# Twelve weight sums made in another part of a batch, with their loads at another place in the DMA queue

## The chip, the core and the metric

One core of a Trainium2 chip runs the whole program. The metric is the device time of one launch in microseconds. In the texts PE is TensorE (PEld its weight loads), DVE is VectorE, ACT is ScalarE, POOL is GpSimd and SP is SyncE, whose queue issues all the DMA transfers of this kernel.

## What is computed

Four batches of causal attention with a memory term, then two gated blocks of matrix products without any nonlinearity between the first block's last two matrices:

```python
scores = scale * q @ k.T, causal; a = softmax(scores); local = a @ v
mem = (phi(q) @ M_prev) / (phi(q) @ z_prev)
x  = g * mem + (1 - g) * local            # [2304, 512], 576 rows a batch
h  = (x @ w1) * (x @ w2)                  # 512 -> 1024
x2 = h @ (w3 @ w_out)                     # 1024 -> 512; the product W' of the two is made once
h  = sigmoid(x2 @ w_gate) * (x2 @ w_val)  # 512 -> 1536
y  = h @ w_out2                           # 1536 -> 512
```

## The kernel before, in words

A batch goes through four stages of matrix products on PE, and each stage is named by the tile in PSUM that it fills: `ab` (x @ w1 and x @ w2), `xw` (h @ W'), the gate stage (`gv` in batch 0, `gvp` in the others) and `ot` (the last product). `ab` runs over eight groups of 128 columns of h (f = 0 to 7), `xw` over four groups d, the gate over twelve, `ot` over four. Each 32-bit operand is split in a high and a low part and every product is made of three matmuls. While PE works on the products of batch b, the attention of batch b + 1 is laid between them: scores (`s`), softmax rows `p` in five row blocks i for each of four head pairs, transposes (`t`), and the products with v and the memory (`o`). In a name such as p2_0_1_0 the numbers are batch, head pair, row block, head. A row block goes from PE (`s`) to DVE (the row minimum and the masked copy, line 724), ACT (exp, line 107), DVE (reciprocal of the sum, lines 747 and 748), DVE and POOL (scaling, line 750, one head each) and back to PE (`t`, line 780), which then has ACT copy the transposed block out of PSUM. In `ab`, DVE multiplies the two halves of h (`hraw`, line 519), and ACT and DVE or POOL split the result into `h`.

The weights go through a ring of five slots (`wslot`). In batch 0 they are converted from 64 bits, and the split weights are stored to HBM (`k<-wslot`, line 328). From batch 1 on `load_step` loads them from there (`wslot<-k`, line 297); a load waits until PE has used up the slot's last weights.

In batches 1 to 3 the gate stage uses a scheme that multiplies sums of weight blocks: `two_rows` takes four slots for each of its twelve column groups, two of which hold sums that have to be made once. That is the making: for each of the twelve groups `load_kept` loads the raw weights that were kept in HBM (`wagain<-kf`, line 249, 512 KB, one of three buffers), and `make_step` makes four adds and subtractions on DVE (lines 265 to 268, 128 x 256 each), and then, for each of two halves, a cast on ACT and a subtraction on DVE (`wmade`, lines 456 and 458) and a store (`s<-wmade`, line 276). The gate stage of batch 1 loads the first sum right after the weights of `xw`. Making happens in batch 1 alone.

`pump`, which every stage calls once for each group of six matmuls or so, moves all this on: one step of conversion, one of loading or splitting, and, in batch 1 (`phase["n"] == 2`), at every second call one step of the making. The first of these steps loads the first three raw blocks at once; when a sum is finished, the load of the third next is issued. Whatever is left is made ahead of the last group of `xw`.

PE's instructions stand in the order in which the program is written. On DVE, ACT, POOL and SP the framework's scheduler sets the order when the program is built, by priority (the order of writing) and by its own idea of when an instruction's inputs are there; on the chip each engine then works strictly in that order, and SP issues its transfers in order too. Such an order puts instructions of the making ahead of the place where they were written when it believes the engine to be free. So the first `wagain` loads stand in SP's queue while PE is still at `ot` of batch 0.

Of the kernel before, what the change touches and what calls it, by code (L numbers as in the profile page):

```python
# [7 lines left out]
F32 = mybir.dt.float32  # L8
# [44 lines left out]
def tile_attention_memory_ffn(  # L53
# [17 lines left out]
    nc = tc.nc  # L71
# [21 lines left out]
    def lower(share):  # L93
        owed[share] = owed.get(share, 0.0) + share[phase["n"]]
        if owed[share] >= 1.0:
            owed[share] -= 1.0
            return nc.gpsimd
        return nc.vector
# [28 lines left out]
    kept = {}  # L127
# [45 lines left out]
    makes = [x[2] for x in seven[1::4]]  # L173
# [9 lines left out]
    ws = {"conv": 0, "step": 0, "split": 0, "ring": 0, "freed": 0, "use": 0, "again": 0, "mstep": 0, "pumps": 0, "wo": 0, "pass": 0, "wready": False}  # L183
    tmp = {}

    last = {}
# [56 lines left out]
    fresh = {}  # L243
    made = set()

    def load_kept(k):
        if k < len(makes):
            t = fp.tile([128, 8, 128], F32, tag="wraw", name=f"wagain{k}", bufs=3)
            nc.sync.dma_start(out=t, in_=kept[makes[k]])
            fresh[k] = t  # L250

    def make_step():


        k = len(made)
        if k >= len(makes):
            return False
        if ws["mstep"] == 0:
            if k == 0:
                assert not raws  # L260
                for n in range(3):
                    load_kept(n)
            a11, a12, a21, a22 = (fresh[k][:, 2 * n : 2 * n + 2] for n in range(4))
            e1, e2 = lower(SHARE_S), lower(SHARE_S)
            e1.tensor_add(a22, a21, a22)
            e2.tensor_sub(a21, a11, a21)
            e1.tensor_sub(a11, a22, a11)
            e1.tensor_sub(a12, a12, a11)
            ws["mstep"] = 1
            return True  # L270
        m = ws["mstep"] - 1
        t = fp.tile([128, 2, 4, 128], F32R, tag="r64", name=f"wmade{k}_{m}", bufs=R64)
        src = fresh[k].rearrange("p (a b) c -> p a (b c)", b=2)
        src = src[:, 0::3] if m == 0 else src[:, 1:3]
        split_rows(t.rearrange("p x (a b) c -> p x a (b c)", b=2), src, SHARE_W)
        nc.sync.dma_start(out=summed[makes[k]][m], in_=t.bitcast(F32))
        ws["mstep"] = (ws["mstep"] + 1) % 3
        if m == 1:
            made.add(makes[k])
            del fresh[k]  # L280
            load_kept(k + 3)
        return True

    def load_step():
        m = ws["again"]
        if m >= len(again):
            return False
        src, nb, u = again[m]
        late = m - NSECOND
        tag, bufs = ("wslot", RING) if late < 0 or late % (RING + 3) < RING else ("wraw", 3)  # L290
        if sum(places[x] == tag for x in slots) >= bufs:
            return False
        while u is not None and u not in made:
            make_step()
        n = ws["ring"]
        w = fp.tile([128, 2, 4, 128], F32R, tag=tag, name=f"wslot{n}", bufs=bufs)[:, :, :nb]
        nc.sync.dma_start(out=w.bitcast(F32), in_=src)
        slots[n] = w
        places[n] = tag
        ws["ring"] += 1  # L300
        ws["again"] += 1
        return True

    def split_step():
        s = ws["split"]
        if s >= 2 * NU:
            return load_step()
        if s >= ws["conv"]:
            return False
        u, hf = divmod(s, 2)  # L310
        r = raws[u][:, 4 * hf : 4 * hf + 4, :]
        if not units[u][1]:
            if ws["wo"] == 4 and ws["pass"] == 0:
                return False
            m = ws["wo"]
            t = fp.tile([128, 2, S], F32R, tag=f"h{8 + m % 4}", name=f"wo{m}", bufs=1)
            wot[m] = t
            split_rows(t[:, :, :DM].rearrange("p x (a c) -> p x a c", c=128), r, SHARE_W)
            ws["wo"] += 1
        else:  # L320
            if ws["ring"] >= ws["freed"] + RING:
                return False
            n = ws["ring"]
            w = fp.tile([128, 2, 4, 128], F32R, tag="wslot", name=f"wslot{n}", bufs=RING)
            split_rows(w, r, SHARE_W)
            if s in stored:
                nb = stored[s].shape[2]
                nc.sync.dma_start(out=stored[s], in_=w[:, :, 4 - nb :].bitcast(F32))
            slots[n] = w
            places[n] = "wslot"  # L330
            ws["ring"] += 1
        if hf == 1:
            del raws[u]
        ws["split"] += 1
        return True

    def pump():
        conv_step()
        split_step()
        if phase["n"] == 2:  # L340
            ws["pumps"] += 1
            if ws["pumps"] % 2 == 0:
                make_step()

    def need(store, s):
# [66 lines left out]
    def two_rows(s, x, name, ht, hraw):  # L412
# [4 lines left out]
        def product(n, sl, blk, xo):  # L417
            ps = ps_f.tile([128, 512], F32, tag="f", name=f"{name[:2]}p{name[2:]}_{n}")[:, :HS]
            prod2(ps, slot(s + sl), blk, x[xo])
            pump()  # L420
            return ps
# [33 lines left out]
    def split_rows(dst, src, share=None):  # L455
        nc.scalar.copy(dst[:, 0], src)  # L456
        eng = lower(share) if share else nc.vector
        eng.tensor_sub(dst[:, 1], src, dst[:, 0].bitcast(F32))  # L458

    def prep(g):  # L460
# [6 lines left out]
        for f in (f0, f0 + 1):  # L467
            s = take(1)
            if p == 1:
                part = fp.tile([128, DM], F32, tag="hraw", name=f"wpart{f}")  # L470
                nc.sync.dma_start(out=part, in_=wp[:, f])
            ps = ps_f.tile([128, 512], F32, tag="f", name=f"wps{p}_{f}")
            for m in range(4):
                prod(ps, slot(s), m, wot[4 * p + m], 0, m == 0, m == 3, n=DM)
                pump()
                yield 5.3
            release(s)
            if p == 0:
                st = fp.tile([128, DM], F32, tag="hraw", name=f"wst{f}")
                nc.scalar.copy(st, ps)  # L480
                nc.sync.dma_start(out=wp[:, f], in_=st)
            else:
                nc.vector.tensor_add(part, ps, part)
                nc.sync.dma_start(
                    out=wd[:, :, f, :], in_=part.rearrange("p (k c) -> p k c", c=128)
                )
# [5 lines left out]
    def ffn(b):  # L492
# [34 lines left out]
        for d in range(KC):  # L527
            while b == 1 and d == KC - 1 and make_step():
                pass
# [525 lines left out]
```

## Time and profile before

| | us |
|---|---|
| median of three runs | 1082.76 |
| fastest and slowest of them | 1078.57, 1084.03 |
| the profiled execution | 1079.02 |
| its span, first instruction to last | 1077.2 |

The profile is of one execution, 1079.02 us long, of which the span of 1077.2 us is what the rows below divide up. Batch 1's `ab` begins at 403.44 us of the span and its `xw` at 490.82. A row of a timeline merges instructions of one line that follow each other; the value in brackets is the idle time of the engine before the row, with what the profile holds for its releaser. Where an engine waited for several things, the profile names the one that came last, and where that one had long been done it was another. A row's time includes the pipeline's tail, so rows that follow each other can overlap.

### The profile page before, as it was taken

The numbers are of one execution on the slowest core, as the hardware profiler recorded it, in microseconds if no ns is written. First come the engines' busy times: TensorE is split into PE (matmuls) and PEld (weight loads), VectorE is DVE, ScalarE is ACT, GpSimd is POOL, SyncE is SP. The second block draws the span as 40 slices with busy tenths as digits, with TensorE's granted clock in tenths as the row PEclk, the third lists the DMA queues.
The fourth block names the chain that finished last, engine by engine and source line by source line (L and its number), as shares of the span: only waits on it lengthen the run. The fifth ranks groups of instructions, "written<-read, shape, count | busy, mean of one in ns | idle before, by whom it ended". The sixth has DMA issues, their size and how long they took to land.

```text
span 1077.2 us, 20188 instructions
## 1 busy us (share of the span) xinstructions
PE 1037.2 (96%) x7400; PEld 922.1 (86%) x7400; DVE 566.3 (53%) x1359; ACT 547.4 (51%) x1188; POOL 429.8 (40%) x373
## 2 busy tenths in 40 slices
PE   7999889999999998999999999999999999999998
PEld 3555667888999897888899899889999899999998
DVE  6854867755557557884555404453566301216630
ACT  7876767657767734564533424454544412224420
POOL 6966656426567602332533212332434200034320
PEclk9999999999999999999999999999999999999999
DMA  8674787858999589994688555433599455548981
GB/s 281 206 232 135 221 284 252 268 198 294 312 331 340 192 295 385 338 333 136 215 303 306 195 161 178 143 105 121 191 318 338 133 154 186 171 150 296 326 288 54
DMA packets 92667, 252.13 MB, mean 234 GB/s; under 512 B 11544, under 2 KB 30104, under 8 KB 92568
## 3 DMA queue, kind: packets, MB, share of 16 engines
q1 hardware_dynamic: 92568, 250.84, 68.3%
q8 instruction: 59, 0.97, 0.4%
q14 instruction: 40, 0.33, 0.1%
HBM read 194.70 MB, written 56.10 MB: 233 GB/s over the span
## 4 chain that ended last, share of the span: by engine, by line
PE 67%; DMA 6%; DVE 3%; POOL 2%; issue 2%; ACT 1%; SPq 1%; POOLq 0%; DVEq 0%; ACTq 0%
PE ab L372 17%; PE gvp L383 15%; PE ot L372 11%; PE xw L372 9%; PE gv L372 4%; PE s L719 3%; PE t L780 3%; PE o L848 2%; DMA wslot<-s 2%; DMA wagain<-kf 1%; PE o L833 1%; POOL x L458 1%; DMA wslot<-k 1%; PE o L841 1%; POOL wraw L234 1%
## 5 line engine op out<-in xcount | busy, mean ns | idle before, releaser
L372 PE MATMUL ab<-x,wslot 128*128 128x288 f32 x1536 | 232.6, 303 | 6.2 <-ACT asb L516 3.1
L372 PEld LDWEIGHTS ab<-x,wslot 128*128 128x128 f32 x1536 | 210.6, 191 | 18.2 <-issue 10.2
L383 PE MATMUL gvp<-x,wslot 128*128 128x288 f32 x1512 | 205.6, 296 | 7.8 <-POOL x L458 3.6
L383 PEld LDWEIGHTS gvp<-x,wslot 128*128 128x128 f32 x1512 | 202.1, 188 | 10.9 <-POOL x L458 4.5
L750 POOL TENSOR_SCALAR p<-p,sm,omg 116x116 f32<-116x116 f32 (+4 forms) x100 | 87.8, 881 | 203.5 <-DVE sm L748 139.6
L372 PE MATMUL ot<-hg,wslot 128*128 128x288 f32 x1152 | 163.4, 298 | 1.4 <-DVE hg L458 1.3
L372 PEld LDWEIGHTS ot<-hg,wslot 128*128 128x128 f32 x1152 | 154.1, 188 | 7.9 <-issue 5.1
L107 ACT ACTIVATE p<-p,sm 116x116 f32<-116x116 f32 (+4 forms) x160 | 93.2, 583 | 66.8 <-DVE sm L724 65.3
L724 DVE CUSTOM_DVE_ANT_0 p<-s,msk 116x116 f32<-116x116 f32 (+4 forms) x160 | 68.2, 453 | 108.5 <-PE s L719 108.3
L234 POOL TENSOR_TENSOR wraw<-wraw,cr 128x512 int32<-128x512 int32 x76 | 110.0, 1461 | 29.6 <-DVE wraw L230 27.9
L372 PE MATMUL xw<-h,wslot 128*128 128x288 f32 x768 | 111.6, 299 | 1.2 <-DVE h L458 0.9
L372 PEld LDWEIGHTS xw<-h,wslot 128*128 128x128 f32 x768 | 103.3, 188 | 4.9 <-issue 2.5
L372 PE MATMUL gv<-x,wslot 128*128 128x288 f32 x576 | 78.4, 296 | 2.0 <-DVE hgraw L584 1.4
L372 PEld LDWEIGHTS gv<-x,wslot 128*128 128x128 f32 x576 | 76.6, 188 | 3.6 <-DVE hgraw L584 2.5
L780 PE MATMUL t<-idf,p 116*116 116x116 f32 x480 | 71.0, 276 | 6.5 <-ACT qts L813 2.2
L780 PEld LDWEIGHTS t<-idf,p 116*116 116x116 f32 x480 | 55.6, 141 | 22.1 <-POOL p L750 5.8
L519 DVE TENSOR_TENSOR hraw<-ab,asb 128x288 f32<-128x288 f32 x64 | 29.2, 456 | 77.7 <-PE ab L372 71.9
L458 POOL TENSOR_TENSOR wslot<-wraw,wslot 128x512 fp32r<-128x512 f32 x36 | 47.4, 1316 | 54.3 <-ACT wslot L456 52.4
L221 ACT ACTIVATE cy<-r 128x512 f32<-128x512 f32 x76 | 50.1, 673 | 25.1 <-DVE wraw L230 10.1
L433 POOL TENSOR_TENSOR u4gv<-u2gv,s5gv 128x288 f32<-128x288 f32 x36 | 30.1, 836 | 69.5 <-ACT s5gv L431 69.5
L222 ACT ACTIVATE cr<-r 128x512 int32<-128x512 uint32 x76 | 50.9, 671 | 12.3 <-POOL wraw L234 11.7
L458 DVE TENSOR_TENSOR wslot<-wraw,wslot 128x512 fp32r<-128x512 f32 x40 | 48.6, 1214 | 15.9 <-ACT wslot L456 13.0
(108 smaller groups left out, 1459.4 us busy)
## 6 DMA issues: line engine op xcount, KB each, us to landing
wslot<-k SPq DMA_DIRECT2D x144, 512.0 KB, 4.4
wslot<-s SPq DMA_DIRECT2D x72, 512.0 KB, 4.6
k<-wslot SPq DMA_DIRECT2D x48, 512.0 KB, 4.4
r<-in_gv_dram SPq DMA_DIRECT2D x24, 512.0 KB, 5.5
s<-wmade SPq DMA_DIRECT2D x24, 512.0 KB, 6.1
qk<-in_qk_dram SPq DMA_DIRECT2D x32, 290.0 KB, 4.3
wslot<-k SPq DMA_DIRECT2D x36, 256.0 KB, 3.9
r<-in_w3t_dram SPq DMA_DIRECT2D x16, 512.0 KB, 4.7
```

The source lines that it names most:

```text
L107: ins = nc.scalar.activation(**kw)
L221: nc.scalar.activation(out=y, in_=hi, func=AF.Prelu, scale=2.0**-112, alpha=2.0**32)
L222: nc.scalar.activation(out=r, in_=w[:, :, 0].bitcast(U32), func=AF.Copy, scale=2.0**-29)
L234: nc.gpsimd.tensor_tensor(z, z, tmp["r"], ALU.add)
L372: nc.tensor.matmul(ps, w[:, wi, blk, :], x[:, xi, cols : cols + n], start=first and part == 0, stop=last and part == 2,)
L383: nc.tensor.matmul(ps, w[:, wi, blk + k, :], x[:, xi, k, :], start=k == 0 and part == 0, stop=k == 1 and part == 2,)
L433: nc.gpsimd.tensor_add(u4, u2, s5)
L458: eng.tensor_sub(dst[:, 1], src, dst[:, 0].bitcast(F32))
L719: nc.tensor.matmul(os_[hh], q_[r, 0, i * T : (i + 1) * T], k_[r, 1, c0:c1], start=x == 0, stop=x == len(terms) - 1,)
L724: nc.vector.tensor_tensor_reduce(out=ps_[hh][:, c0:c1], in0=os_[hh], in1=msk[:, SP - w + c0 : SP - w + c1], scale=-0.125, scalar=3.0e38 if ...
L750: lower(SHARE_N).tensor_scalar(ps_[hh][:, :w], ps_[hh][:, :w], sm[:, 6 + hh : 7 + hh], omg[:T, 2 * p + hh : 2 * p + hh + 1], ALU.mult, ALU ...
L780: nc.tensor.transpose(tp[:T, c : c + T], src[hh][:, j * T : (j + 1) * T], idf[:T, :T])
```

## The change

Three things are changed in the making, and nothing in what is computed. The step is called at 39 of the 88 calls of `pump` in batch 1's `ab` and the first three groups of `xw`, evenly, where it was every second call. The first three loads are steps of their own, one a step (39 = 3 + 12 x 3). And a making load is tied behind the latest ring load (`issue_after`), so that it stands after it in SP's queue.

```diff
     def load_kept(k):
         if k < len(makes):
             t = fp.tile([128, 8, 128], F32, tag="wraw", name=f"wagain{k}", bufs=3)
-            nc.sync.dma_start(out=t, in_=kept[makes[k]])
+            with tc.issue_after(last["ring"].ins):
+                nc.sync.dma_start(out=t, in_=kept[makes[k]])
             fresh[k] = t
...
         if ws["mstep"] == 0:
-            if k == 0:
+            if len(fresh) < 3 and k == 0:
                 assert not raws
-                for n in range(3):
-                    load_kept(n)
+                load_kept(len(fresh))
+                return True
...
-        nc.sync.dma_start(out=w.bitcast(F32), in_=src)
+        last["ring"] = nc.sync.dma_start(out=w.bitcast(F32), in_=src)
...
             ws["pumps"] += 1
-            if ws["pumps"] % 2 == 0:
+
+            if ws["pumps"] * 39 // 88 > (ws["pumps"] - 1) * 39 // 88:
                 make_step()
```

How the built order moves is seen at three places. In the names the number after a tile's own is the program's count of allocations, and lines after line 249 are one or two higher in the changed kernel.

SP's queue where batch 0 ends and batch 1's `ab` gets its first weights. Here `out_0_dram` is batch 0's result, `k79` and the like are split weights on their way to HBM, and `wslot76` and `wslot77` are the first two slots of `ab`. Before:

```order
L328 DMA k82_179<-wslot74_4635 128x1024
L249 DMA wagain2_4853<-kf26_121 128x1024
L276 DMA s25_0_117<-wmade1_0_5002 128x1024
L249 DMA wagain3_4929<-kf27_126 128x1024
L276 DMA s25_1_118<-wmade1_1_5021 128x1024
L297 DMA wslot76_4709<-k18_85 128x1024
L328 DMA k83_180<-wslot75_4693 128x1024
L249 DMA wagain4_5025<-kf28_131 128x1024
L297 DMA wslot77_4723<-k19_86 128x1024
L604 DMA out_0_dram<-osb0_2_4641 128x576
```

And in the changed kernel, from the same store on:

```order
L329 DMA k82_179<-wslot74_4635 128x1024
L298 DMA wslot76_4709<-k18_85 128x1024
L329 DMA k83_180<-wslot75_4693 128x1024
L298 DMA wslot77_4723<-k19_86 128x1024
L606 DMA out_0_dram<-osb0_2_4641 128x576
L298 DMA wslot78_4779<-k22_87 128x1024
L298 DMA wslot79_4793<-k23_88 128x1024
L298 DMA wslot80_4807<-k26_89 128x1024
L606 DMA out_0_dram<-osb0_3_4727 128x576
L250 DMA wagain0_4865<-kf24_111 128x1024
L250 DMA wagain1_4902<-kf25_116 128x1024
```

All five ring loads and the last store of batch 0 now stand ahead of the first making load, where there were five making loads and four stores of half sums ahead of the second ring load.

DVE in the first column group of batch 1's `ab`, from the product of the first half of h to the scaling of the second softmax row block (`p2_0_1_0`), for which PE's transposes wait. Before, the last nine rows of that stretch:

```order
L657 TENSOR_SCALAR me2_1_5289<-qnr2_1_5223 116x640
L748 RECIPROCAL sm2_0_1_4880<-sm2_0_1_4880 116x2
L265 TENSOR_TENSOR wagain5_5125<-wagain5_5125 128x256
L666 RECIPROCAL mn2_0_4839<-mn2_0_4839 116x10
L724 ISA p2_0_2_0_4937,sm2_0_2_4939<-s2_0_2_0_0_4940,msk_82 116x348
L724 ISA sm2_0_2_4939 116x1
L724 ISA p2_0_2_1_4938,sm2_0_2_4939<-s2_0_2_0_1_4941,msk_82 116x348
L724 ISA sm2_0_2_4939 116x1
L750 TENSOR_SCALAR p2_0_1_0_4878<-p2_0_1_0_4878,sm2_0_1_4880,omg_84 116x232
```

The same rows in the changed kernel:

```order
L659 TENSOR_SCALAR me2_1_5265<-qnr2_1_5205 116x640
L266 TENSOR_TENSOR wagain1_4902<-wagain1_4902 128x256
L268 TENSOR_TENSOR wagain0_4865<-wagain0_4865 128x256
L750 RECIPROCAL sm2_0_1_4872<-sm2_0_1_4872 116x2
L668 RECIPROCAL mn2_0_4839<-mn2_0_4839 116x10
L726 ISA p2_0_2_0_4921,sm2_0_2_4923<-s2_0_2_0_0_4924,msk_82 116x348
L726 ISA sm2_0_2_4923 116x1
L726 ISA p2_0_2_1_4922,sm2_0_2_4923<-s2_0_2_0_1_4925,msk_82 116x348
L726 ISA sm2_0_2_4923 116x1
L267 TENSOR_TENSOR wagain1_4902<-wagain1_4902 128x256
L269 TENSOR_TENSOR wagain0_4865<-wagain0_4865 128x256
L752 TENSOR_SCALAR p2_0_1_0_4870<-p2_0_1_0_4870,sm2_0_1_4872,omg_84 116x232
```

The whole stretch held one half sum (`wmade4_0`) and one add of `wagain5`; it now holds four adds of `wagain0` and two of `wagain1`, the first right behind `hraw1_0`. From that scaling on, up to the first instruction of the fifth row block (`p2_0_4_0`), there were seven adds and three half sums, and now there are ten and seven.

DVE late in `ab`, from the end of column group 6 on: `hraw1_6` is the product of its second half, `mphi2_2` belongs to the memory term, `p2_2_1` is the second row block of the third head pair. In the kernel before the twelfth sum stands ahead of `hraw1_6`, and none behind it. In the changed kernel:

```order
L521 TENSOR_TENSOR hraw1_6_5646<-ab1_6_1_1_5731,asb1_6_1_5729 128x288
L752 TENSOR_SCALAR p2_2_0_0_5746<-p2_2_0_0_5746,sm2_2_0_5748,omg_84 116x116
L662 SCALAR_TENSOR_TENSOR mphi2_2_5763<-qnr2_2_5700,me2_2_5762 116x640
L266 TENSOR_TENSOR wagain9_5744<-wagain9_5744 128x256
L267 TENSOR_TENSOR wagain9_5744<-wagain9_5744 128x256
L268 TENSOR_TENSOR wagain9_5744<-wagain9_5744 128x256
L269 TENSOR_TENSOR wagain9_5744<-wagain9_5744 128x256
L666 TENSOR_REDUCE mn2_2_5764<-me2_2_5762 116x10
L726 ISA p2_2_1_0_5829,sm2_2_1_5831<-s2_2_1_0_0_5832,msk_82 116x232
```

The tenth and the eleventh sum (`wagain9`, `wagain10`) now stand between the end of column group 6 and `h1_7`, the last part of h, and the twelfth stands in the second group of `xw`. On SP the load of `wagain9` comes right behind that of `wslot93`.

## Rows read from the trace of the kernel before

**Rows 1.** The page, busy time: share of the span, instructions.

```profile
PE 1037.2 (96%) x7400; PEld 922.1 (86%) x7400; DVE 566.3 (53%) x1359; ACT 547.4 (51%) x1188; POOL 429.8 (40%) x373
```

**Rows 2.** Windows: length; PE, PEld, DVE, ACT, POOL busy; granted clock, DMA share, GB/s.

```profile
400.00:410.00 10.00, 6.95 (x48) 6.20 (x47) 5.69 (x18) 2.67 (x10) 0.00 (x0) 0.95 1.02 404
410.00:420.00 10.00, 8.88 (x61) 7.89 (x61) 9.82 (x30) 5.90 (x17) 3.23 (x3) 0.88 1.03 415
420.00:430.00 10.00, 10.00 (x78) 9.14 (x78) 7.75 (x20) 6.08 (x14) 2.44 (x2) 1.00 0.94 351
```

**Rows 3.** Timeline of PE: start, length, line, operands, count, idle before and releaser.

```profile
399.84 2.96 PE L372 MATMUL ot<-hg,wslot 128*128 128x288 f32 x21
403.44 0.64 PE L372 MATMUL ab<-x,wslot 128*128 128x288 f32 x3 [0.65 <-DMA wslot<-k]
...
408.30 1.93 PE L372 MATMUL ab<-x,wslot 128*128 128x288 f32 x9 [2.40 <-DMA wslot<-k]
...
417.29 0.59 PE L780 MATMUL t<-idf,p 116*116 116x116 f32 x4 [1.12 <-ACT p L107]
...
444.53 0.28 PE L780 MATMUL t<-idf,p 116*116 116x116 f32 x1 [0.46 <-DVE p L750]
445.54 0.32 PE L780 MATMUL t<-idf,p 116*116 116x116 f32 x1 [0.73 <-POOL p L750]
```

**Rows 4.** The chain of waits in order of time: start, length, what.

```profile
398.59 9.57 DMA wslot<-k
...
490.82 3.16 PE xw L372 x24
```

**Rows 5.** Timeline of SP, the issues: start, length of the issue, line, operands.

```profile
394.31 0.32 SPq L249 DMA_DIRECT2D wagain<-kf  x1
394.68 1.44 SPq L276 DMA_DIRECT2D s<-wmade  x1
396.21 0.39 SPq L297 DMA_DIRECT2D wslot<-k  x1
...
397.63 0.86 SPq L249 DMA_DIRECT2D wagain<-kf  x1
398.59 0.96 SPq L297 DMA_DIRECT2D wslot<-k  x1
...
474.34 0.33 SPq L297 DMA_DIRECT2D wslot<-k  x1
```

**Rows 6.** The tile `wagain`: duration min/median/max in ns; last, landings in us.

```profile
L458 DVE TENSOR_TENSOR wmade<-wagain,wmade x24: 679/692/1470, 383.4 to 476.9; 128x512 fp32r<-128x512 f32 x24
...
L265 DVE TENSOR_TENSOR wagain<-wagain x12: 400/424/1669, 381.4 to 465.7; 128x256 f32<-128x256 f32 x12
...
DMA to landing us min/median/max: 4.4/7.5/10.5
```

**Rows 7.** Timeline of DVE, first column group of `ab`.

```profile
413.17 0.45 DVE L519 TENSOR_TENSOR hraw<-ab,asb 128x288 f32<-128x288 f32 x1
...
416.75 0.39 DVE L750 TENSOR_SCALAR p<-p,sm,omg 116x232 f32<-116x232 f32 x1
```

**Rows 8.** Windows, the making's instructions on DVE (two rows); then all engines.

```profile
374.00:403.00 29.00, 10.74 (x23) 1.00 0.82 298
403.00:480.00 77.00, 30.44 (x50) 0.98 0.95 350
...
403.00:480.00 77.00, 71.86 (x540) 63.75 (x542) 64.53 (x170) 44.70 (x106) 22.49 (x17) 0.98 0.95 350
```

**Rows 9.** Timelines of DVE and of POOL, one instruction each.

```profile
433.63 1.67 DVE L265 TENSOR_TENSOR wagain<-wagain 128x256 f32<-128x256 f32 x1
...
432.99 2.02 POOL L637 TENSOR_TENSOR qkl<-qk,qkh 128x580 fp32r<-128x580 f32 x1 [6.13 <-PE t L780]
```

**Rows 10.** Timeline of DVE, last column group of `ab`.

```profile
477.97 0.82 DVE L660 SCALAR_TENSOR_TENSOR mphi<-qnr,me 116x640 f32<-116x640 f32 x1
...
489.06 0.52 DVE L724 CUSTOM_DVE_ANT_0 p<-s,msk 116x348 f32<-116x348 f32 x1 [4.51 <-PE s L719]
...
492.13 0.77 DVE L458 TENSOR_TENSOR h<-hraw,h 128x576 fp32r<-128x576 f32 x1
```

## The prediction

> **What bounds the kernel now.** I read the engines' busy times first: TensorE is busy for 96% of the span [rows 1], so only time in which it stands still, or runs slowly, can be won or lost. Then I looked for such time where the diff acts, around the start of batch 1's x @ W stage (the tile `ab`). The ten-microsecond windows show it: PE busy is 6.95 of 10 us from 400 us on and 8.88 in the next ten, and the granted clock falls to 0.95 and 0.88 there, while DMA is full (1.02, 1.03) and DVE is at 9.82 of 10 in the second [rows 2]. The timeline of TensorE gives the waits one by one: 0.65 and 2.40 us for the ring's first two slots, 1.12 us before the transposes of the second softmax row block, and later 0.46 and 0.73 us before those of the next head pair [rows 3]. The row with 1.12 names an ACT instruction; the DVE row that writes `p` ends at 417.14, just before, so I take DVE as the releaser [rows 7]. The chain of waits goes through a ring load that took 9.57 us from issue to landing [rows 4], and SyncE's timeline tells why: making traffic (`wagain<-kf`, `s<-wmade`) is issued just before and between the ring loads [rows 5].
>
> **The change part by part.** No instruction of any engine is added or removed; twelve sums are still made, each with six DVE instructions, two ACT casts, one load and two stores. What changes is when.
>
> *The ring's first loads go ahead of all making traffic* (first excerpt of the order). That takes away the waits of 0.65 and 2.40 us: the loads are then issued as PE frees the slots, with no making traffic among them. It also takes away what followed the 2.40 us: granted shares of 0.95 and 0.88 over ten us each mean (0.05 + 0.12) x 10 x 2 = 3.4 us at the lower level of 1.2 GHz, which cost half, 1.7 us. Term A: -3.05 - 1.7 = -4.75 us. I see no way for much less: the second of these slots is freed one group of output columns before `ot` ends, 72 products at 2.96 / 21 = 0.14 us or 10 us [rows 3], and even a landing of 7.5 us fits in.
>
> *The first sums now meet the first softmax blocks on DVE.* Before, four sums were started before PE came to `ab`. Now `wagain0` is issued behind the last ring load and the last output store. PE ends `ot` at 399.84 + 2.96 = 402.80 [rows 3]; I allow 0.9 us for the copy of the last output and the issues, so 403.7. Its landing I bound by the making loads of before, 4.4 us at least and 7.5 in the median [rows 6]: 408.1 to 411.2, and I take the middle, 409.7, as less is in flight than when the median was measured. In DVE's order (second excerpt) four adds of `wagain0` and two of `wagain1` now stand between `hraw` and the scaling of `p2_0_1_0`. Before, that stretch took 417.14 - 413.17 = 3.97 us [rows 7], of which some 0.36 is `hraw`, 0.60 one half sum and 0.32 one add (start to start); 2.7 are left, and six adds at 0.42 plus gaps make 2.7 more [rows 6]: 5.4 us from landing. The block is ready at 413.5 to 416.6, middle 415.1. PE comes there at 402.80 + (417.29 - 403.44) - 2.40 - 1.12 - 1.7 = 411.4. So it waits 2.2 to 5.3 us, middle 3.8, where it waited 1.12: +2.7 (1.1 to 4.2). A wait of 2.40 us was followed by the lower clock, one of 1.12 was not a cause of its own [rows 2, 3]; a wait of 3.8 should cost the 1.7 us again (0 to 1.7). Term B: +4.4 us (1.1 to 5.9). This is the heart of the forecast: the stall moves from a ring slot to a softmax block.
>
> *The next twelve us.* From the scaling of `p2_0_1_0` to the first instruction of the fifth block, DVE's order had seven adds and three half sums, and now has ten adds and seven half sums: 3 x 0.42 + 4 x 0.69 = 4.0 us more [rows 6]. DVE had 10 - 7.75 = 2.25 us idle in the window that holds most of this [rows 2]. So it comes 1.8 us late if all the idle time can be filled, 4.0 if none can, and 0 if PE has slack there that no row shows. PE had no wait there. Term C: +2.0 us (0 to 4.0), near the lower of the two delays, as DVE's idle time lies between short waits that the adds can fill.
>
> *Later blocks.* At the second head pair the order of DVE had an add of `wagain8` and a long step between the sums and the scaling; now the scaling goes first. The waits of 0.46 and 0.73 us end. Term D: -1.2 us (-1.2 to 0).
>
> *Loads behind the ring's.* From here each `wagain` load stands in SyncE's queue behind a ring load that waits for PE, and DVE meets its adds soon after (third excerpt). For `wagain9`: the ring load `wslot93` was issued at 474.34 [rows 5], so `wagain9` at about 474.8; DVE comes to the adds when `mphi` ends, 478.8 [rows 10]: 4.0 us, less than the shortest landing, 4.4 [rows 6]. It stands 0.4 to 3.5 us, and behind the adds on DVE wait the softmax blocks, `hraw` and `h1_7`, for which PE waits at the first columns of h @ W'. In that stretch DVE also gets two sums that it didn't have, 8 x 0.42 + 4 x 0.69 = 6.1 us, against an idle time of 4.51 us before the third block [rows 10]. Late by 6.1 + 0.4 - 4.5 = 2.0 to 6.1 + 3.5 - 4.5 = 5.1 us, of which `h1_7` can take some 1.5: it ended at 492.90, and the last of the eight products that PE does first there runs to 490.82 + 3.16 = 493.98 [rows 4, 10]. Term E: +1.8 us (0 to 3.6). The same happens at `wagain7` with more slack; Term F: +0.7 us (0 to 2), an estimate at a third of E.
>
> *What costs nothing.* The last sum is now stored just before `wslot99`'s load, which waits for PE anyway, and `wslot101`, the first load of a sum, is two ring loads later; nobody waits for a store. The steps of x2 that set the end of the xw stage come after the last half sum in DVE's and ACT's order, so their waits of before stay. Batches 2 and 3 keep their order.
>
> Sum: -4.75 + 4.4 + 2.0 - 1.2 + 1.8 + 0.7 = **+2.95 us**. All lower ends added give -4.85, all upper ones with D at 0 +10.75.
>
> *POOL beside DVE.* An add of `wagain` that overlapped a POOL instruction of 2.02 us took 1.67 us instead of 0.42 and ended 0.3 us after it [rows 9]. Six making instructions on DVE took 10.74 / 23 x 6 = 2.8 us before 403 us and 30.44 / 50 x 6 = 3.65 after [rows 8], where POOL is at work. The four sums that move there may each cost 0.85 us more, 3.4 in all; I count it within the upper ends of C, E and F. The Trainium skill (GPSIMD Engine Reference, Specifications) says that GpSimd shares its SBUF interfaces with VectorE and contends with VectorE instructions that have two SBUF inputs; every making instruction is one. The rule speaks against this change, and the two rows agree with it; by it the sum moves by up to those 3.4 us, to some +6.35.
>
> **The rivals.**
> *DVE keeps up (faster).* `wagain0` lands early, the making lags behind the softmax, and the late loads delay nobody: A and D hold, B is at its lower end, C, E and F are 0. That is -4.75 + 1.1 - 1.2 = -4.85, and -6 if the wait of 1.12 us goes too. For it: DVE is busy for 64.5 of 77 us from 403 to 480 [rows 8], not full, and it held the same pace of a sum in about 8 us there with few stalls of PE. Against: an engine works in order, and the excerpts show adds ahead of softmax steps. It needs `wagain0` to land within 4.4 us.
> *DVE becomes the bound (slower).* Making on DVE from 403 to about 500 us is twelve sums at 3.65 us = 44 us, with other work of 64.5 - 30.4 = 34 us per 77, or 43 per 97: 87 of 97 us, 90%, against 84% before [rows 8]. Place: blocks 2 to 5 of head pairs 0 and 1, and `h1_7`. Price: B, C, E and F at their upper ends with A and D, -4.75 + 5.9 + 4.0 - 1.2 + 3.6 + 2 = +9.55. It decides when a `wagain` load lands later than some 6.5 us in most sums; half of those of before took over 7.5 [rows 6].
> *It doesn't spread.* The name says evenly; the order places three loads at once and four sums in the first two of the eight columns. If that alone mattered, B and C would be all: -4.75 + 4.4 + 2.0 - 1.2 = +0.45.
>
> **How the numbers follow.** The profiled execution took 1079.02 us, 3.7 below the median of the three runs, 1082.76. The sum is made on the former (1082.0); on the median it is 1085.7, which I give, +0.3%. A difference under 0.5% (5.4 us) is about what a measurement of this kernel can't tell from none. Chances: forecast, within -3 and +5.4 us with the third rival in it, 0.60; DVE keeps up 0.13 (0.09 of it beyond 0.5%); DVE bound 0.27. So faster 0.09, same 0.64, slower 0.27. The range leaves out some 0.05 of the faster rival below it and 0.15 of the slower one above, and goes from -4.8 to +8.2 us: 1078 to 1091.
>
> **What would show it.** In the changed kernel's profile: no wait of PE for `wslot<-k` at the first columns of `ab`, and ring loads that land within 7 us; a wait of some 2 to 5 us before the transposes of the second block, with DVE idle just before for `wagain<-kf`, and the clock low after it; small waits within the next 15 us; no wait at the first block of the second head pair; a wait of 1 to 3 us for `h1_7`. Wrong if the second block comes without a wait over 1.2 us (then faster), if PE's waits from 403 to 500 us exceed 12 us (slower), or if the stage of the gate changes at all.

## The result, and the profile after

The changed kernel took 1086.51 us in the median of 17 executions (1081.76 to 1090.2), the kernel before beside it 1080.78 (1077.82 to 1085.42, 17 executions). The ratio of the two, which is not taken from the medians, is 1.0062, 95% interval [1.0043, 1.0080]: some 6.7 us slower (the medians lie 5.7 us apart), a little more than the 0.5% that the prediction took as the least that can be told, with an interval that reaches below it. The profiled execution took 1081.76 us with a span of 1080.0, against 1079.02 and 1077.2.

The page's busy line and TensorE's waits from 365 to 530 us (engine, line and operation that waited, releaser, us in total, times, longest). They answer to [rows 1] and [rows 3]:

```profile
PE 1038.9 (96%) x7400; PEld 924.6 (86%) x7400; DVE 561.4 (52%) x1359; ACT 548.2 (51%) x1188; POOL 430.7 (40%) x373
...
PE t L782 <- DVE mn L669: 3.4, 1, 3.4
PE s L721 <- DVE sm L726: 2.5, 1, 2.5
PE gvp L385 <- POOL x L460: 0.8, 1, 0.8
PE xw L374 <- ACT h L458: 0.8, 1, 0.8
PE xw L374 <- DVE h L460: 0.5, 1, 0.5
```

The ring's waits of 0.65 and 2.40 us are gone. Their place is taken by two long waits for DVE and two short ones for `h1_7`, all downstream of the making of the sums. The windows, in the columns of [rows 2], show where the clock falls now:

```profile
400.00:410.00 10.00, 8.81 (x69) 7.66 (x67) 5.65 (x22) 3.87 (x13) 2.69 (x2) 1.00 0.99 316
410.00:420.00 10.00, 7.79 (x48) 7.30 (x49) 10.00 (x31) 5.07 (x11) 3.57 (x2) 0.83 0.76 263
...
460.00:470.00 10.00, 7.46 (x43) 6.45 (x43) 7.11 (x18) 4.33 (x9) 1.46 (x1) 0.73 0.88 301
470.00:480.00 10.00, 10.00 (x75) 9.77 (x75) 6.55 (x19) 6.44 (x16) 2.42 (x4) 0.92 0.65 195
```

From 410 us the granted clock is 0.83, that is 0.17 x 20 = 3.4 us at the lower level of 1.2 GHz, behind a wait of 3.40 us. From 460 us it is 0.73 and 0.92, or (0.27 + 0.08) x 20 = 7.0 us at that level, behind a wait of 2.54 us. In [rows 2] the fall stood at 400 and 410 us, and from 460 us on the kernel before had none:

```profile
460.00:470.00 10.00, 10.00 (x82) 9.33 (x81) 8.76 (x28) 6.50 (x14) 1.48 (x1) 1.00 0.81 249
```

How each wait comes about is read from three timelines. TensorE, at the second softmax block, at the second half of the scores of the second head pair's fifth block (`s2_1_4` in what follows), and at the first columns of h @ W' (start, length, line, operands, count, idle before and releaser):

```profile
412.20 0.58 PE L782 MATMUL t<-idf,p 116*116 116x116 f32 x4 [3.40 <-DVE mn L669]
...
465.72 0.96 PE L721 MATMUL s<-qkh 64*116 64x290 f32 x2 [2.54 <-DVE sm L726]
...
495.02 0.53 PE L374 MATMUL xw<-h,wslot 128*128 128x288 f32 x2 [0.80 <-ACT h L458]
496.03 0.40 PE L374 MATMUL xw<-h,wslot 128*128 128x288 f32 x1 [0.48 <-DVE h L460]
```

For the first wait the profile names the writing of `mn` as the releaser. The transposes read `p`, whose scaling DVE ends just before it, at 411.66 + 0.39 = 412.05 us. DVE ahead of these waits, with the first add of `wagain0` and of `wagain7`:

```profile
405.03 0.46 DVE L521 TENSOR_TENSOR hraw<-ab,asb 128x288 f32<-128x288 f32 x1
407.36 0.42 DVE L266 TENSOR_TENSOR wagain<-wagain 128x256 f32<-128x256 f32 x1 [1.87 <-DMA wagain<-kf]
...
411.66 0.39 DVE L752 TENSOR_SCALAR p<-p,sm,omg 116x232 f32<-116x232 f32 x1
...
458.83 0.46 DVE L521 TENSOR_TENSOR hraw<-ab,asb 128x288 f32<-128x288 f32 x1 [0.92 <-PE ab L374]
462.57 0.42 DVE L266 TENSOR_TENSOR wagain<-wagain 128x256 f32<-128x256 f32 x1 [3.28 <-DMA wagain<-kf]
...
465.20 0.45 DVE L726 CUSTOM_DVE_ANT_0 p<-s,msk 116x290 f32<-116x290 f32 x1
```

And SyncE's issues of the same two loads, each behind ring loads (at the first place the last store of batch 0's result stands between them):

```profile
397.25 3.52 SPq L298 DMA_DIRECT2D wslot<-k  x3
...
401.30 0.91 SPq L250 DMA_DIRECT2D wagain<-kf  x2
...
453.94 0.32 SPq L298 DMA_DIRECT2D wslot<-k  x1
454.32 0.93 SPq L250 DMA_DIRECT2D wagain<-kf  x1
```

The reader is to see one pattern twice. A ring load waits for TensorE to free a slot; the making's load stands behind it and goes out only then (401.30, 454.32). It lands 6.0 and 8.2 us later, and DVE, which takes its instructions in order, comes to the add first and stands (1.87 and 3.28 us). What TensorE needs is queued on DVE behind the add: the scaling of `p` at 411.66, and at 465.20 the reading of the last scores, behind which TensorE writes the next ones. At the first place the late load is only a part of it: from `hraw` to the scaling DVE took 411.66 - 405.03 = 6.6 us and stood for 1.87 of them, and six adds stand in the rest. With the load in time TensorE would still have waited 3.40 - 1.87 = 1.5 us, by an estimate. The tile `wagain` as a whole, the idle time of DVE for its loads (us, times) and its landings (us, min/median/max), beside [rows 6]:

```profile
  DMA wagain<-kf: 7.0, 3
...
DMA to landing us min/median/max: 6.0/7.0/9.3
```

The landings are no worse than before in the median (7.0 against 7.5 us). Nor is it new that DVE stands for such loads. In the kernel before it did so four times, for 14.1 us in all, the last time within `ab`:

```profile
  DMA wagain<-kf: 14.1, 4
```

```profile
407.00 0.42 DVE L265 TENSOR_TENSOR wagain<-wagain 128x256 f32<-128x256 f32 x1 [3.36 <-DMA wagain<-kf]
```

Three of these waits lay before 403 us, where TensorE waited for nothing of DVE's, and the last ended while TensorE itself stood for a ring slot, until 408.30 us [rows 3]. What is new is the work that stands on DVE behind the adds. The Trainium skill (DMA: Bandwidth & Descriptors, Anatomy of one DMA — SWDGE (gpsimd) path) gives a fit of 2.0 us plus the bytes by 436 KB per us for one DMA of another issue path; for the 512 KB of a `wagain` tile that would be an estimate of 3.2 us. No `wagain` load landed in under 6.0 us in this profile of the changed kernel (5.1 in a second one), with the DMA engines 0.65 to 0.99 busy in the windows above, so the measurement decides.

### The profile page after: what moved, and what is told of

Same layout as the page of the kernel before. It is cut to its first block, busy times and chain, and to the rows that moved or that the text cites. A ratio compares the mean times of both kernels' runs of the same rounds, so it can differ in the third digit from the quotient of the medians.

```text
span 1080.0 us, 20186 instructions
## 1 busy us (share of the span) xinstructions
PE 1038.9 (96%) x7400; PEld 924.6 (86%) x7400; DVE 561.4 (52%) x1359; ACT 548.2 (51%) x1188; POOL 430.7 (40%) x373
## 4 chain that ended last, share of the span: by engine, by line
PE 70%; DMA 4%; DVE 4%; POOL 2%; issue 2%; ACT 1%; SPq 0%; POOLq 0%; DVEq 0%; ACTq 0%
PE ab L374 16%; PE gvp L385 16%; PE ot L374 14%; PE xw L374 9%; PE gv L374 5%; PE s L721 3%; PE t L782 3%; PE o L850 2%; DMA wagain<-kf 2%; DMA wslot<-s 1%; PE o L835 1%; POOL x L460 1%; POOL wraw L234 1%; PE o L843 1%; PE qt L819 1%
```

## The experiments

The theory: what the change wins at the ring it loses, and more, by DVE standing for late loads with softmax work queued behind. The main rival: DVE simply has too much work once twelve sums fall into the stage, however it is queued. In the table, "timed" is the ratio to the kernel before with its interval. "Stretch" is read from TensorE's timeline: from the first product of batch 0's last stage (`ot`) to the first product of the second half of `xw` (behind the wait for `h1_7`), less 140.6 us, the mean of three executions of the kernel before (142.30, 139.60, 140.02; the last two are experiments below). "To the end" is the same from `ot` to the end of the span, less the mean of 723.0 us; it takes in batch 1's gate stage, which uses the sums. For the experiments both are of one execution each, while "timed" is of five to ten.

| kernel | timed | in us | stretch | to the end |
|---|---|---|---|---|
| changed (two executions in the last two columns) | 1.0062 [1.0043, 1.0080] | +6.7 | +6.5, +7.1 | +6.9, +7.0 |
| early_rest_tied | 1.0056 [1.0022, 1.0089] | +6.0 | +3.9 | +4.8 |
| tie_first3 | 1.0030 [1.0002, 1.0057] | +3.2 | +1.3 | +2.2 |
| early3 | 0.9975 [0.9947, 1.0003] | -2.7 | -1.0 | -1.3 |
| no_work | 0.9954 [0.9924, 0.9984] | -5.0 | -6.4 | -5.4 |
| tie_only | 1.0053 [1.0029, 1.0077] | +5.7 | +1.3 | +3.7 |
| adds_later | 0.9967 [0.9952, 0.9982] | -3.6 | -5.7 | -4.4 |
| p34 | 0.9975 [0.9958, 0.9992] | -2.7 | -4.2 | -4.3 |
| adds_later_early3 | 0.9967 [0.9945, 0.9988] | -3.6 | -6.0 | -3.9 |

**Which late loads cost what.** Three kernels make four corners with the changed one: the first three loads late or early, the rest late or not (in early3 loads 3 and 4 stay late). In `load_kept` of the changed kernel, the tie to the ring is made conditional:

```diff
     def load_kept(k):
...
-            with tc.issue_after(last["ring"].ins):
+            if k >= 3:            # early_rest_tied;  early3: k in (3, 4);  tie_first3: k < 3
+                with tc.issue_after(last["ring"].ins):
+                    nc.sync.dma_start(out=t, in_=kept[makes[k]])
+            else:
                 nc.sync.dma_start(out=t, in_=kept[makes[k]])
```

> The changed kernel, but its first three wagain loads are not tied to the ring any more (so they go out in batch 0's last stage, as in the kernel before); loads 3 to 11 stay tied. Theory (DVE, in order, stands for late wagain loads): the wait of 3.4 us before the second softmax block goes, with the lower clock after it; the wait of some 2.5 us at s2_1_4 for wagain7, with the lower clock after it, and the 1 to 2 us for h1_7 stay. So 3 to 5 us less than the changed kernel, about the time of the kernel before: ratio 0.999 to 1.002. Rival (DVE has too much work after 403 us, however it is queued): three sums fewer there, the waits at s2_1_4 and h1_7 go too; ratio 0.995 to 0.997.

TensorE's waits there from 365 to 530 us:

```profile
PE s L724 <- DVE sm L729: 2.8, 1, 2.8
PE ab L377 <- ACT asb L521: 1.9, 1, 1.9
PE xw L377 <- DVE h L463: 0.5, 1, 0.5
PE xw L377 <- ACT h L461: 0.8, 1, 0.8
```

The mechanism came out as expected: the wait at the second softmax block is gone, those at `s2_1_4` (2.8 us) and for `h1_7` (0.8 and 0.5) are as in the changed kernel. The ratio, 1.0056, was above the expected 0.999 to 1.002, and its interval doesn't tell it from the changed kernel's; the trace of one execution shows +3.9 us in the stretch against +6.5 and +7.1. A wait that nobody had foreseen may account for the miss: 1.9 us for an `asb` copy of ACT.

> The changed kernel with only wagain3 and wagain4 tied to the ring; the first three loads go out in batch 0's last stage, and from wagain5 on a load goes out as soon as its buffer is free. Theory (late loads): both long waits of DVE go, at the second softmax block and at s2_1_4, and the one for h1_7; what the ring won stays. 1075 to 1077.5 us, ratio 0.995 to 0.997, with PE's waits from 400 to 500 us under 3 us. Rival (ring order must hold through the stage, or DVE is full): ring loads wait again behind making traffic, or the softmax blocks wait for DVE at other places; ratio 0.999 or more.

The same wait is in this kernel, and it is all that is left for the making there. SyncE, DVE, ACT and TensorE at that place, one after the other, and the window:

```profile
420.15 1.92 SPq L301 DMA_DIRECT2D wslot<-k  x2
422.12 0.42 SPq L251 DMA_DIRECT2D wagain<-kf  x1
```

```profile
429.49 0.52 DVE L269 TENSOR_TENSOR wagain<-wagain 128x256 f32<-128x256 f32 x1 [3.33 <-DMA wagain<-kf]
...
430.63 0.51 DVE L729 CUSTOM_DVE_ANT_0 p<-s,msk,sm 116x290 f32<-116x290 f32 x1
```

```profile
431.24 0.78 ACT L107 ACTIVATE p<-p,sm 116x580 f32<-116x580 f32 x1 [3.09 <-DVE sm L729]
```

```profile
434.56 1.09 PE L377 MATMUL ab<-x,wslot 128*128 128x288 f32 x6 [1.93 <-ACT asb L521]
```

```profile
430.00:440.00 10.00, 8.07 (x48) 7.49 (x48) 10.00 (x30) 6.64 (x16) 1.21 (x1) 0.77 0.97 368
```

It is the third instance of the pattern: `wagain4` is tied behind two ring loads, DVE stands 3.33 us for it, ACT waits for DVE's `sm` before its exponentials, and the copy that frees TensorE's PSUM buffer is queued behind these on ACT. The waits at `s2_1_4` and `h1_7` are gone, as the theory said and the rival for full DVE did not: both kernels have three sums made early and the same work left, and they differ by 6.0 + 2.7 = 8.7 us timed, with intervals that don't meet. The ratio, 0.9975, is just above the expected 0.995 to 0.997, by much less than its interval; that wait would account for it.

> The changed kernel with only the first three wagain loads tied to the ring; loads 3 to 11 go out as soon as their buffer is free. Theory (late loads): the wait of 3 to 5 us at the second softmax block stays, since its load is as late; the waits at s2_1_4 and h1_7 go. 5 to 7 us less than the changed kernel at those two places, against up to 3 us of new small waits, as the sums come faster there: ratio 0.999 to 1.002. Rival (DVE has too much work): no gain over the changed kernel, ratio 1.005 or more, with waits for DVE at other softmax blocks.

TensorE's two longest waits:

```profile
PE t L785 <- DVE mn L672: 3.4, 1, 3.4
PE t L785 <- DVE p L755: 1.1, 1, 1.1
```

The wait at the second softmax block is the same 3.4 us, since its load is as late; those at `s2_1_4` and for `h1_7` are gone, with 1.1 us at another block's transposes (447 us) and 0.6 us at the scores of the first head pair (432 us). At 1.0030 the time is just above the expected 0.999 to 1.002 and below the rival's 1.005, but its interval reaches both; what speaks against the rival here is the trace.

**What the work alone costs.**

> The changed kernel without the making's work on DVE and ACT: each wagain tile is loaded and stored twice as it is, so the loads, stores and their bytes stay, and the sums are not made (the later batches multiply with other numbers). Theory (DVE stands, TensorE waits for DVE): all waits of TensorE from 403 to 500 us go that are not of the products themselves, with the lower clock: 1073.5 to 1076.5 us, ratio 0.993 to 0.996. Rival (the making's traffic, not its work, delays the ring and the stores): TensorE still waits for ring slots; ratio 0.999 or more.

The adds, the casts and the subtractions of the making are left out:

```diff
-            e1.tensor_add(a22, a21, a22)
-            e2.tensor_sub(a21, a11, a21)
...
-        split_rows(t.rearrange("p x (a b) c -> p x a (b c)", b=2), src, SHARE_W)
-        nc.sync.dma_start(out=summed[makes[k]][m], in_=t.bitcast(F32))
+        nc.sync.dma_start(
+            out=summed[makes[k]][m], in_=fresh[k].rearrange("p (x a) c -> p x a c", x=2)
+        )
```

The sum line of its windows from 390 to 510 us:

```profile
sum 120.00, PE 120.00 PEld 108.33 DVE 54.21 ACT 54.80 POOL 34.74; mean PE 10.00 PEld 9.03 DVE 4.52 ACT 4.57 POOL 2.90
```

TensorE was busy for the whole 120 us, at a granted clock of 1.00 throughout; 0.9954 lies within the expected band. So the making's loads and stores, put behind the ring's, delay nothing by themselves in this stretch. About 5 us below the kernel before, with an interval of 1.7 to 8.2, is an estimate of the most that another order of the making can give.

**The two parts of the change.** The new pace alone, without the tie, is built to the same order of instructions on every engine as the kernel before; there was nothing to run. The tie alone, here against the changed kernel:

```diff
-            if ws["pumps"] * 39 // 88 > (ws["pumps"] - 1) * 39 // 88:
+            if ws["pumps"] % 2 == 0:
                 make_step()
...
-            if len(fresh) < 3 and k == 0:
-                load_kept(len(fresh))
-                return True
+            if k == 0:
+                for n in range(3):
+                    load_kept(n)
```

> One part of the change alone: the wagain loads tied to the ring, with the pace and the three loads at once of the kernel before (the other part alone, the pace, gives the very order of the kernel before on every engine, so there is nothing to run). Theory (late loads): the wait at the second softmax block stays at 3 to 5 us, and so does the wait for a late wagain load later on, wherever the order puts it: ratio 1.002 to 1.007. Rival (the spread to the last columns is what costs, as it puts sums on DVE beside the last softmax blocks and h1_7): no wait near s2_1_4 and h1_7, ratio 0.999 to 1.002.

```profile
PE t L781 <- DVE p L751: 3.7, 1, 3.7
...
PE s L720 <- DVE sm L725: 0.8, 1, 0.8
```

The first wait stays, as expected. The second that the theory expected is short, 0.8 us at 435 us, and nothing is left at `s2_1_4` and `h1_7`, as the rival had it. The time, 1.0053, is that of the theory. Timing and trace don't quite agree here: the stretch shows +1.3 us, and 5.7 were timed. A part of the rest lies behind the stretch: to the end the trace shows +3.7 us. In batch 1's gate stage, from 530 to 610 us, TensorE waits 4.7 us for `wslot<-s`, the loads of the sums, against 1.3 to 2.0 us in the three executions of the kernel before. Why these loads come later was not followed. So the waits at `s2_1_4` and `h1_7` belong to the changed pace together with the tie, but how much of the 6.7 us the pace adds is not settled: the intervals of the two kernels overlap almost wholly.

**The same late loads, with DVE's order changed.** This run decides. Loads, stores, ties and work are those of the changed kernel, and each making load still stands behind the same ring load; only the first add of each sum is queued on DVE behind the last `hraw` product written before it:

```diff
-            e1.tensor_add(a22, a21, a22)
+            with tc.issue_after(last["hraw"].ins):
+                e1.tensor_add(a22, a21, a22)
...
-                nc.vector.tensor_mul(hraw[:, c0 : c0 + HS], pss[1][:, :HS], asb)
+                last["hraw"] = nc.vector.tensor_mul(hraw[:, c0 : c0 + HS], pss[1][:, :HS], asb)
```

> The changed kernel, in which the first add of every sum is queued on DVE behind the last hraw product written before it in the program; loads, stores, their ties and the amount of work are as in the changed kernel. Theory (DVE stands in order for a late load, and what is queued behind the add waits): the loads land as late as before, 6 to 9 us, but DVE has other work until then: no wait of TensorE at the second softmax block or at s2_1_4 over 1 us, no fall of the clock from 400 to 500 us: 3 to 7 us less than before the change's losses, ratio 0.994 to 0.998. Rival (DVE has too much work, or the late loads hold back something else than DVE): the waits move and keep their sum, ratio 1.002 or more.

The landings, DVE at the second softmax block (where the scaling of `p` now stands ahead of the first add), and the windows in the columns of [rows 2], with the sum line of the five windows from 400 to 430 and from 460 to 480 us, first of the changed kernel, then of this one:

```profile
DMA to landing us min/median/max: 5.0/7.2/9.1
```

```profile
408.82 0.40 DVE L753 TENSOR_SCALAR p<-p,sm,omg 116x232 f32<-116x232 f32 x1
...
411.60 0.41 DVE L267 TENSOR_TENSOR wagain<-wagain 128x256 f32<-128x256 f32 x1
```

```profile
410.00:420.00 10.00, 10.00 (x80) 9.47 (x79) 9.56 (x27) 7.51 (x18) 1.37 (x2) 1.00 0.84 309
420.00:430.00 10.00, 10.00 (x79) 9.33 (x78) 9.43 (x23) 6.44 (x13) 4.22 (x3) 1.00 0.98 356
...
470.00:480.00 10.00, 10.00 (x80) 6.98 (x78) 9.93 (x24) 4.19 (x12) 3.72 (x3) 1.00 0.95 364
```

```profile
sum 50.00, PE 44.03 PEld 39.97 DVE 37.13 ACT 26.93 POOL 11.46; mean PE 8.81 PEld 7.99 DVE 7.43 ACT 5.39 POOL 2.29
```

```profile
sum 50.00, PE 50.00 PEld 44.63 DVE 43.68 ACT 30.32 POOL 16.61; mean PE 10.00 PEld 8.93 DVE 8.74 ACT 6.06 POOL 3.32
```

The loads take as long to land as in the changed kernel (7.2 us in the median), DVE is busier in these five windows (43.68 of 50 us for 37.13), and TensorE does not wait in them: 50.00 of 50 us at a clock of 1.00. Up to the gate stage its only waits are 0.5 us for a scaling of `p` on POOL and 0.3 us for `h1_7`. The ratio went from 1.0062 to 0.9967, as expected. That shows the cause and excludes the rival: neither the amount of work nor the lateness of the loads costs much by itself, but the place of the adds in DVE's order, ahead of steps that TensorE needs. How much of that is DVE standing and how much the adds' own time, this run does not divide. This kernel is also faster than both.

**Early sums and later adds together.** Two kernels take both steps: the first three sums early, `wagain3` tied to the ring's slot 80, all other making loads untied, and the first adds moved back for sums 3 and 4 (p34) or 3 to 11 (adds_later_early3). p34 also goes back to a step at every second call of `pump`, and begins sums 3 and 4 not before its calls 16 and 24.

```diff
-            with tc.issue_after(last["ring"].ins):
+            if k == 3:
+                with tc.issue_after(rings[80].ins):
...
-            e1.tensor_add(a22, a21, a22)
+            if k in (3, 4):       # adds_later_early3: k >= 3
+                with tc.issue_after(last["hraw"].ins):
+                    e1.tensor_add(a22, a21, a22)
```

> The first three sums early, in batch 0's last stage; wagain3 tied to the ring load of slot 80, the others untied; the adds of sums 3 and 4 on DVE behind the last hraw product. Theory: what is left of waits in the run with three early sums (1.93 us of TensorE for an asb copy behind a wait of DVE for wagain4, and the lower clock after it) goes, and the gain of the ring's first loads stays: ratio 0.994 to 0.997. Rival: DVE then lacks time later, with waits of 1 to 3 us at the last softmax blocks: ratio 0.998 or more.

> The first three sums early, in batch 0's last stage; wagain3 tied to the ring load of slot 80, the others untied; the first adds of sums 3 to 11 on DVE behind the last hraw product written before them. Theory: no wait of TensorE for DVE from 400 to 500 us, close to the run without the making's work: ratio 0.993 to 0.997. Rival: the sums end too late, and the stage of x2 or the ring's loads of the sums wait for them: ratio 0.998 or more, with a wait at about 540 us.

p34 gave 0.9975, half a thousandth above its band, adds_later_early3 0.9967; neither is better than adds_later. The long waits for DVE are gone in both; p34 has one of 1.5 us for an ACT copy instead. All three lie 1.4 to 2.3 us above no_work, within the intervals, and that rest was not followed further.

**Whether one profile is typical.** In all kernels timed until then, the timed difference was larger than the one between their trace and the first trace of the kernel before, counted from `ot` to the end, so that trace itself came under suspicion.

> The kernel before, unchanged, for a second profiled execution. In all nine kernels so far the timed difference from the kernel before lies 0.4 to 3.8 us (mean 2.4) above the difference that the traces show from batch 0's last stage to the end. If the first profiled execution of the kernel before was one with long ring waits (0.65 and 2.40 us with 1.7 us of lower clock after them), this one shows some 2 us less of them in that stage: TensorE from the start of batch 0's last stage to the start of x @ W's successor (xw of batch 1) 135.5 to 137 us instead of 138.2. Rival (the ring waits are the same in every execution, and the difference lies elsewhere): 138 us again, with the waits at the same places.

> The same once more, a third profiled execution: as for the second. If the two new ones differ by over 1.5 us in that stage, the waits for the ring are a matter of chance from one execution to the next.

TensorE's waits of over 0.5 us from 398 to 416 us, in the second execution and then in the third, beside [rows 3]:

```profile
406.14 1.42 PE L372 MATMUL ab<-x,wslot 128*128 128x288 f32 x9 [0.58 <-DMA wslot<-k]
...
415.17 0.58 PE L780 MATMUL t<-idf,p 116*116 116x116 f32 x4 [2.09 <-ACT p L107]
```

```profile
406.52 1.43 PE L372 MATMUL ab<-x,wslot 128*128 128x288 f32 x9 [2.10 <-DMA wslot<-k]
...
414.43 0.58 PE L780 MATMUL t<-idf,p 116*116 116x116 f32 x4 [1.51 <-ACT p L107]
```

From `ot` to the first product of `xw` they took 135.5 and 135.9 us, as expected, against 138.2 in the first. The ring's waits are 0.58 and 2.10 us in place of 0.65 + 2.40, and the granted clock is 1.00 from 400 to 430 us in both. The wait for the second softmax block was longer in exchange, 2.09 and 1.51 us for 1.12. So what the change could win at the ring was smaller in these two than in the one on which the prediction rests.

> The changed kernel, unchanged, for a second profiled execution. Theory: its waits come from the order (a load issued behind a ring load that waits for TensorE), not from chance: again 3 to 4 us before the second softmax block, 2 to 3.5 us at s2_1_4, 1 to 2 us in all for h1_7, each of the first two with the lower clock after it, and 140 to 144 us for the same stretch. Rival (the wait at s2_1_4 was chance, its load having landed late, 8.23 us): under 1 us there, and 136 to 138.5 us for the stretch.

Its waits came again at the same places: 3.7 us at the second block, 2.8 us at `s2_1_4`, 0.8 and 0.5 us for `h1_7`, and 141.9 us from `ot` to the first product of `xw`, against 141.3 in the first. So they come from the order, not from chance. From the mean of three (140.6) to the mean of two (147.4) the change costs 6.8 us up to the second half of `xw`: as much as was timed (6.7 by the ratio, 5.7 by the medians).

## Why the prediction was right, and where it was not

The time lay in the range (1078 to 1091) and 0.8 us from the forecast of 1085.7, but that closeness is partly luck: the basis of 1082.76 was 2.0 us above the median of 17, and the change cost 5.7 us by the medians (6.7 by the ratio), not 2.95. By the bound of 0.5% the likeliest class was "same"; the result lies just beyond, on the slower side, with an interval that covers both. Of its signs, no wait at the ring (its loads landed in 3.2 to 6.1 us), the wait at the second block with the lower clock, none at the second head pair's first block and 1.28 us for `h1_7` came, and TensorE's waits of 3.40, 2.54, 0.80 and 0.48 us stayed under the 12 us that would have spoken against it. The small waits within the next fifteen us did not come, and the wait at `s2_1_4` was not among the signs. Term by term, from TensorE's starts in the two profiled executions:

- **A (ring's waits and the clock), -4.75: measured -4.9.** Right for the profile that it was read from. In the two later executions of the kernel before there was less to win, 0.58 or 2.10 us with no lower clock. What failed here is to carry a wait of one execution over to the median as if it were fixed.
- **B (second softmax block), +4.4: measured +3.7.** The wait was 3.40 us for a forecast of 3.8, the landing 6.0 us after issue, the middle of the bounds, and DVE took 4.7 us from there to the end of the scaling, not 5.4. The clock did fall again. The mechanism held, 0.7 us smaller than forecast, and it was the heart of the forecast.
- **C (the next twelve us), +2.0: measured +0.4.** Over-sized. DVE is busy for 10.00 of 10 us there and late, but no block of that stretch was needed sooner.
- **D (second head pair), -1.2: measured -1.6.** Right, a little beyond the end of its range.
- **E (`wagain9`, `h1_7`), +1.8: measured +1.8** (waits of 0.80 and 0.48 us and what follows them). Right, though the slack of 1.5 us that it took is 493.98 - 492.90 = 1.1 us by the two rows that it gives.
- **F (`wagain7`), +0.7: measured +5.4.** This is the step that failed, far outside its range of 0 to 2 us. It was put "at a third of E" on the ground of "more slack", with no row for the slack. There was none: DVE stood 3.28 us, TensorE waited 2.54 us for the reading of the scores, and some 7 us at the lower clock followed, 2.8 us of loss. That term alone is 4.7 us off; the five others together are 2.8 us off the other way.

In sum the first profile shows -4.9 + 3.7 + 0.4 - 1.6 + 1.8 + 5.4 = +4.8 us up to `xw`.

Of the rivals, "DVE keeps up" fell with the first wait. "DVE becomes the bound" named the right side and the right condition (loads that land later than some 6.5 us; the median was 7.0), but the wrong reason: adds_later has the same work and no such wait. "It doesn't spread", by which A to D would be all, fell with E and F, 7.2 us together. The rule of the Trainium skill (GPSIMD Engine Reference, Specifications), that GpSimd contends with VectorE's instructions that have two SBUF inputs, was given up to 3.4 us; the making took 40.0 us of DVE in all after the change and 41.2 before, so nothing of that kind can be seen in the sum, although single adds still took 1.6 us.

## What to carry to other kernels

When a load is moved behind others in a queue, look at the engine that uses it: if it takes its work in order, the cost is not the load's lateness but everything queued behind the first instruction that needs it, and moving that one instruction back can be worth as much as moving the load (here 0.9967 for adds_later, 0.9975 for early3, with intervals that overlap). Each place at which the pattern occurs needs its own row for the slack; a place priced by analogy was here the largest error. And a wait for a DMA in a single profile is a sample: where the first execution waited 3.05 us for the ring, two more waited 0.58 and 2.10.

## What the runs showed of the hardware

The landing of a 512 KB `wagain` load beside busy DMA engines took 3.3 to 10.5 us in the traces of all these kernels, with medians of 6.4 to 8.1, issued behind the ring or not. The fall of the granted clock after a wait was not a matter of the wait's length alone: a wait of 1.93 us (early3, clock 0.77 in that window) and those of 2.40 to 3.7 us named above were followed by it, those of 2.10 and 2.09 us in the two later executions of the kernel before were not (1.00). And DVE at 9.4 to 9.9 of 10 us busy, in windows of adds_later in which TensorE was busy throughout, shows that a nearly full engine need not be a bound.
